# A decode layer on one core: key transposes on 4-byte pairs, flat weight loads, and the gate weights on eight DMA engines

## The chip, the cores and the metric

The kernel runs on one core of one Trainium2 chip. The metric is the device time of one execution in microseconds (us). Each kernel is timed beside the kernel before, in the same rounds on the same chip. Kernels of different rounds are compared by their ratios to it, and the text says so.

## The reference

One token of 448 numbers is normalised, attends with 16 query heads to a cache of 8 heads with 65,536 positions of width 256, and goes in parallel through a gated feed-forward block of width 1,792. Everything is bf16.

```python
x  = A_x                                    # 1 x 1 x 448
xn = layernorm(x)
# attention: q = xn @ wq (448 x 4096); each kv head serves two query heads
scores = einsum("bhqd,bhkd->bhqk", q, k) * 256 ** -0.5      # k, v: 8 x 65536 x 256 each
attn   = einsum("bhqk,bhkd->bhqd", softmax(scores), v) @ wo  # wo: 4096 x 448
# feed-forward on the same token
y = (silu(xn @ w_gate) * (xn @ w_up)) @ w_down               # gate, up: 448 x 1792
return x + attn + (xn + y * sigmoid(xn @ w_r))
```

K and V together are 2 x 8 x 65,536 x 256 x 2 bytes = 536.9 MB, out of 549.0 MB read. Every byte is used once, so this is a kernel that reads.

## The kernel before

One queue, issued by SyncE, brings everything into a ring of 172 KB per partition, in the order of a list of items: `wq`, then K and V pieces of 4 MB (64 positions per partition) alternating one head apart, with gate, up, down and `wo` put in between. An item is loaded as soon as the ring space that it overwrites is free. Each 4 MB transfer is cut into 128 packets of 32,768 bytes, one for each partition, and sixteen DMA engines carry eight packets each. The semaphore of an item receives one increment from each engine that carried part of it; the trace keeps the time of each, so every transfer has a vector of sixteen *landings*. An engine's *lag* is its landing less the first one of the same transfer; the *spread* is the largest lag.

```python
def rows_dmas(src, n, off):                 # wq, gate, up: 448 rows = 3 x 128 + 64
    d = []
    if nfull:                               # 384 rows, three to a partition
        d.append((lambda a, s=src: (a[:, off:off + nfull * n].rearrange("p (k n) -> p k n", k=nfull),
                                    s[0:nfull * P, :].rearrange("(k p) n -> p k n", p=P))))
    if rem:                                 # 64 rows on partitions 0-63 only
        d.append((lambda a, s=src: (a[0:rem, off + nfull * n:off + (nfull + 1) * n], s[nfull * P:D, :])))
    return d
# [...]
def v_next():                               # order of the stream
    v = vs.pop(0)
    if v[3] + v[4] == NPP and v[2] < Hkv - 1 or v[2] == Hkv - 1 and v[3] == sum(V_LAST[:WO_LAST]):
        wo_item(v[2])                       # wo rows of a head, ahead of its last V piece
    kv_item(*v)
    if v[2] == 0 and v[3] == 2 * V_CHUNKS[0]:
        item("ffn1", 2 * DK * F, rows_dmas(B_w_gate, F, 0) + rows_dmas(B_w_up, F, DK * F))
# [...]
def pe_T(n, s, m, j):                       # 16 positions x 128 partitions of keys are one set;
    # [...]                                 # a set takes four of these calls
    kv = ap_of(n).rearrange("p (j d) -> p j d", d=Dh)
    for hf in range(NH):                    # NH = 2 halves of the head width
        for jj in range(GN):                # GN = 4
            blk = hf * GN + jj
            ins = nc.tensor.matmul(ps_t[g % NTB][:, blk * P:(blk + 1) * P],
                                   lhsT=kv[:, j + GN * m + jj, hf * P:(hf + 1) * P],
                                   rhs=ident_bf[:, :], is_transpose=True, start=True, stop=True)
# [...]
def pe_QK(s):                               # scores of the set, from the transposed keys
    # [...]
    ins = nc.tensor.matmul(ps_q[32 * m:32 * m + rep, 0:512],
                           lhsT=qT_sb[:, hf, h * rep:(h + 1) * rep],
                           rhs=kt[:, hf * 512:(hf + 1) * 512],
                           start=(hf == 0), stop=(hf == NH - 1), tile_position=(0, 32 * m))
```

TensorE (PE) first transposes the keys (an identity matmul for each 128 x 128 block), VectorE (DVE) and ScalarE (ACT) copy the result out of PSUM, and PE multiplies it with the queries. V needs no transpose.

## Time and profile before

| | before |
|---|---|
| time, median of 3 runs | 1310.78 us (1310.16 to 1310.97) |
| PE, DVE, ACT busy | 70%, 41%, 33% of the span |
| DMA busy | 9 tenths or more in 39 of 40 slices |
| read rate, slices without weights | about 430 GB/s |
| PE instruction fetches | 107 packets of 16 KB |

The page of the profile of before follows, cut. The rows under the busy shares cut the span into 40 equal slices: the digit is the busy tenths, the GB/s what the DMA engines moved. The two queue lines give packets, megabytes and share of the sixteen engines' time. After them comes the chain of waits that ended last, then the costliest group of PE (count, then busy us, mean ns of one, and idle time ahead).

```profile
span 1309.1 us, 29128 instructions
PE 921.8 (70%) x13690; PEld 701.4 (54%) x13690; DVE 537.7 (41%) x885; ACT 426.6 (33%) x555; POOL 4.5 (0%) x34
...
DMA  9999999999999999999999999999999999999995
GB/s 383 426 427 429 415 382 432 430 430 431 431 430 425 432 428 430 431 428 431 430 430 427 429 429 430 430 430 430 428 428 429 428 426 433 429 429 416 434 426 213
...
q8 instruction: 107, 1.75, 0.5%
...
DMA 75%; PE 25%; SPq 0%; issue 0%; DVE 0%
...
L370 PE MATMUL ps_t<-ident_bf,ring 128*128 128x128 bf16 x8192 | 598.1, 241 | 309.8 <-DMA ring<-in_A_k_cache_dram 308.0
```

The DMA row says what bounds the kernel: the engines of the stream never rest, and the chain is DMA for three quarters. PE, at 70%, spends 309.8 us idle ahead of transposes, waiting for keys. So only what the stream itself loses can be won: slices 5 and 6 (gate, up and down, 415 and 382 GB/s), the first slice (`wq`, 383), and the last (213).

The last slice is the largest. The landings explain it. These are the landings of the sixteen engines for the last transfer of the stream (sorted, in us after the first engine):

```
before, last V piece   0.0 0.02 0.12 0.16 0.19 0.22 0.33 2.44 | 15.76 15.79 16.01 16.05 16.31 17.3 17.43 18.07
```

For the first pieces of the stream all sixteen lie within 0.4 us. By the end, eight engines lag 16 to 18 us behind the first. The slow eight are those that also carry PE's instruction fetches: the queue line has 107 packets of 16 KB, and each adds about 1.55 us to the lag of one engine. It can be seen piece by piece: in those that end at 218.1, 227.8, 237.5 and 247.2 us, with one fetch between each and the next, the lags sum to 28.2, 29.6, 31.2 and 32.9 us, and each time one engine of the slow eight has moved. PE's stream has about 27,390 instructions, which is 107 x 256. The Trainium skill ("Runtime: NRT & Kernel Launch", Instruction fetch mechanics) says that instructions are refilled in 16 KiB blocks of 256 instructions; the trace agrees with the size. The page adds that the cost of a block is "mostly hidden". No wait of PE on the page is put down to it ("issue" is 0% of the chain), but the stream, which ends with its slowest engine, does pay.

How PE does one set of transposes, and the end of the chain, in the profile of before (start us, duration us, what, and the number of instructions):

```profile
61.73 0.60 PE L398 MATMUL ps_q<-kt_buf,qT_sb 128*2 128x512 bf16 x8
62.27 1.96 PE L370 MATMUL ps_t<-ident_bf,ring 128*128 128x128 bf16 x32
```

```profile
1258.10 45.19 DMA ring<-in_A_v_cache_dram
1303.33 0.63 PE ps_o L658 x4
1303.98 0.70 DVE ob_sb L511
1305.24 1.66 PE ps_m L557 x4
1306.93 0.61 DVE res_bf L543
```

A set is 32 transposes in 1.96 us. After the last V piece come four matmuls, a cast, and four matmuls with `wo` (L557, 1.66 us).

### The profile page before, as it was taken

The numbers are of one execution on the slowest core, as the hardware profiler recorded it, in microseconds if no ns is written. First come the engines' busy times: TensorE is split into PE (matmuls) and PEld (weight loads), VectorE is DVE, ScalarE is ACT, GpSimd is POOL, SyncE is SP. The second block draws the span as 40 slices with busy tenths as digits, with TensorE's granted clock in tenths as the row PEclk, the third lists the DMA queues.
The fourth block names the chain that finished last, engine by engine and source line by source line (L and its number), as shares of the span: only waits on it lengthen the run. The fifth ranks groups of instructions, "written<-read, shape, count | busy, mean of one in ns | idle before, by whom it ended". The sixth has DMA issues, their size and how long they took to land.

```text
span 1309.1 us, 29128 instructions
## 1 busy us (share of the span) xinstructions
PE 921.8 (70%) x13690; PEld 701.4 (54%) x13690; DVE 537.7 (41%) x885; ACT 426.6 (33%) x555; POOL 4.5 (0%) x34
## 2 busy tenths in 40 slices
PE   5998765867866767667767668667677577676444
PEld 5886654645645645555556556456456455555210
DVE  3776432434524534335334344345344353353100
ACT  2666322333323423324233233233233242333100
POOL 1000000000000000000000000000000000000000
PEclk9999878878879888788788788788788887888666
DMA  9999999999999999999999999999999999999995
GB/s 383 426 427 429 415 382 432 430 430 431 431 430 425 432 428 430 431 428 431 430 430 427 429 429 430 430 430 430 428 428 429 428 426 433 429 429 416 434 426 213
DMA packets 24701, 550.89 MB, mean 421 GB/s; under 512 B 2371, under 2 KB 6214, under 8 KB 7366
## 3 DMA queue, kind: packets, MB, share of 16 engines
q1 hardware_dynamic: 24578, 549.04, 98.4%
q8 instruction: 107, 1.75, 0.5%
q14 instruction: 12, 0.10, 0.0%
q10 hardware_dynamic: 4, 0.00, 0.0%
HBM read 549.03 MB, written 0.00 MB: 419 GB/s over the span
## 4 chain that ended last, share of the span: by engine, by line
DMA 75%; PE 25%; SPq 0%; issue 0%; DVE 0%
DMA ring<-in_A_k_cache_dram 68%; PE ps_t L370 17%; DMA ring<-in_A_v_cache_dram 7%; PE ps_q L398 4%; PE ps_o L658 2%; PE ps_s L431 1%; PE ps_m L557 0%; SPq L298 0%; PE ps_m L608 0%; PE ps_m L531 0%; DVE ob_sb L511 0%; DVE res_bf L543 0%; PE ps_m L502 0%; DVE oT_sb L518 0%
## 5 line engine op out<-in xcount | busy, mean ns | idle before, releaser
L370 PE MATMUL ps_t<-ident_bf,ring 128*128 128x128 bf16 x8192 | 598.1, 241 | 309.8 <-DMA ring<-in_A_k_cache_dram 308.0
L370 PEld LDWEIGHTS ps_t<-ident_bf,ring 128*128 128x128 bf16 x8192 | 552.0, 110 | 423.8 <-DMA ring<-in_A_k_cache_dram 336.1
L352 DVE COPY kt_buf<-ps_t 128x1024 bf16<-128x1024 bf16 x768 | 493.2, 686 | 636.9 <-PE ps_t L370 636.2
L354 ACT ACTIVATE kt_buf<-ps_t 128x1024 bf16<-128x1024 bf16 x256 | 262.1, 1024 | 431.0 <-PE ps_t L370 430.1
L383 ACT ACTIVATE s<-ps_q 98x512 bf16<-98x512 f32 x256 | 152.9, 597 | 335.5 <-PE ps_q L398 335.5
L658 PE MATMUL ps_o<-ring,S_sb 128*4 128x512 bf16 x2048 | 136.6, 412 | 48.1 <-DMA ring<-in_A_v_cache_dram 46.1
L398 PE MATMUL ps_q<-kt_buf,qT_sb 128*2 128x512 bf16 x2048 | 167.9, 407 | 0.0
L658 PEld LDWEIGHTS ps_o<-ring,S_sb 128*4 128x4 bf16 x2048 | 49.3, 89 | 122.1 <-DMA ring<-in_A_v_cache_dram 54.3
L431 PE MATMUL ps_s<-sel_bf,s 128*128 128x8 bf16 x1024 | 64.9, 169 | 0.7 <-ACT s L383 0.7
L431 PEld LDWEIGHTS ps_s<-sel_bf,s 128*128 128x128 bf16 x1024 | 57.2, 102 | 2.4 <-ACT s L383 1.6
L511 DVE CAST ob_sb<-ps_o 100x512 bf16<-100x512 f32 x8 | 5.5, 692 | 83.7 <-PE ps_o L658 83.7
L398 PEld LDWEIGHTS ps_q<-kt_buf,qT_sb 128*2 128x2 bf16 x2048 | 26.2, 79 | 5.5
L477 ACT ACTIVATE S_sb<-S_sb,negmax 128x512 bf16<-128x512 bf16 x16 | 13.4, 861 | 7.3 <-DVE negmax L470 7.2
L585 PE MATMUL ps_m<-xnT_sb,ring 128*128 128x1 bf16 x112 | 8.1, 175 | 8.8 <-DMA ring<-in_B_w_up_dram 8.8
L585 PEld LDWEIGHTS ps_m<-xnT_sb,ring 128*128 128x128 bf16 x112 | 7.2, 106 | 10.1 <-DMA ring<-in_B_w_up_dram 9.3
L689 PE MATMUL ps_m<-xnT_sb,ring 128*128 128x1 bf16 (+1 forms) x128 | 9.2, 174 | 4.3 <-DMA ring<-in_A_wq_dram 4.3
L411 DVE CAST S_sb<-ps_s 128x512 bf16<-128x512 f32 x16 | 10.9, 682 | 1.3 <-PE ps_s L431 1.3
L413 DVE TENSOR_REDUCE m1p<-S_sb 128x2 f32<-128x512 bf16 x16 | 11.0, 686 | 0.6
L689 PEld LDWEIGHTS ps_m<-xnT_sb,ring 128*128 128x128 bf16 (+1 forms) x128 | 8.3, 106 | 5.3 <-issue 4.4
L557 PE MATMUL ps_m<-ring,oT_sb 128*1 128x448 bf16 x32 | 8.4, 390 | 1.9 <-DVE oT_sb L518 1.9
L502 PEld LDWEIGHTS ps_m<-rowsum,ones_f 128*128 128x128 f32 x32 | 5.8, 256 | 5.1 <-issue 5.1
L570 DVE TENSOR_TENSOR gs_sb<-ps_m,sg_sb 128x14 f32<-128x14 f32 x1 | 0.2, 173 | 18.5 <-ACT sg_sb L565 18.5
(63 smaller groups left out, 62.3 us busy)
## 6 DMA issues: line engine op xcount, KB each, us to landing
ring<-in_A_k_cache_dram SPq DMA_DIRECT2D x63, 4096.0 KB, 44.3
ring<-in_A_v_cache_dram SPq DMA_DIRECT2D x63, 4096.0 KB, 37.9
ring<-in_A_wo_dram SPq DMA_DIRECT2D x8, 448.0 KB, 30.3
ring<-in_A_wq_dram SPq DMA_DIRECT2D x1, 3072.0 KB, 10.4
ring<-in_A_k_cache_dram SPq DMA_DIRECT2D x2, 1024.0 KB, 15.1
ring<-in_A_k_cache_dram SPq DMA_DIRECT2D x1, 2048.0 KB, 21.8
ring<-in_A_v_cache_dram SPq DMA_DIRECT2D x1, 2048.0 KB, 41.6
ring<-in_B_w_down_dram SPq DMA_DIRECT2D x1, 1568.0 KB, 34.4
```

The lines of the kernel that those rows point to most:

```text
L352: op(e, ("EV", g), lambda x: x.tensor_copy(out=kt[:, :], in_=tb[:, :]))
L354: op(e, ("EV", g), lambda x: x.activation(out=kt[:, :], in_=tb[:, :], func=ACTF.Copy))
L370: ins = nc.tensor.matmul(ps_t[g % NTB][:, blk * P:(blk + 1) * P], lhsT=kv[:, j + GN * m + jj, hf * P:(hf + 1) * P], rhs=ident_bf[:, :], is ...
L383: op("act", ("EVQ", s), lambda e: e.activation(out=s2[s % 2][0:QROWS, :], in_=ps_q[0:QROWS, :], func=ACTF.Copy))
L398: ins = nc.tensor.matmul(ps_q[32 * m:32 * m + rep, 0:512], lhsT=qT_sb[:, hf, h * rep:(h + 1) * rep], rhs=kt[:, hf * 512:(hf + 1) * 512], s ...
L411: op("dve", ("SCOPY", b), lambda e: e.tensor_copy(out=S[:, k * SBN:(k + 1) * SBN, :], in_=ps_s[:, :, :]))
L413: op("dve", ("SMAX", b), lambda e: e.tensor_reduce(out=m1p[:, h % 2, :, k], in_=S[:, k * SBN:(k + 1) * SBN, :].rearrange("p n i -> p i n") ...
L431: ins = nc.tensor.matmul(o, lhsT=s2[s % 2][:, jj * P:(jj + 1) * P], rhs=sel_bf[:, :, :], start=True, stop=True)
L477: op("act", ("EXPI", h, i), lambda e, i=i: e.activation(out=S[:, :, i], in_=S[:, :, i], func=ACTF.Exp, bias=negmax[:, h, i:i + 1], scale=1 ...
L585: ins = nc.tensor.matmul(ps_m[0:P, base + f:base + f + 1], lhsT=w[0:r, t, kc, f * P:(f + 1) * P], rhs=xnT_sb[0:r, kc:kc + 1], start=(kc == ...
L658: ins = nc.tensor.matmul(ps_o[32 * g:32 * g + 2 * rep, :], lhsT=S[:, k:k + 2, :].rearrange("p n i -> p (n i)"), rhs=kv[:, j:j + 2, :], sta ...
L689: ins = nc.tensor.matmul(ps_m[0:P, c:c + 1], lhsT=w[0:r, kc, q * Dh + hf * P:q * Dh + (hf + 1) * P], rhs=xnT_sb[0:r, kc:kc + 1], start=(kc ...
```

## The change

The intent is to take work from the DMA stream, and from its slow engines above all. There are four parts.

1. **Transposes on 4-byte pairs** (`t4`). Two neighbouring bf16 keys are treated as one fp32, so one transpose moves a 128 x 256 block instead of two that move 128 x 128 each: 4,096 instead of 8,192. The two halves of the head width become even and odd elements, and the scores matmul reads every second column.
2. **Flat weights** (`flat`). `wq`, gate and up are loaded as one contiguous run for each of 128 partitions (3.5 of the 448 rows each), and `w_down` in runs of two rows. No remainder on half the partitions, and longer packets. PE then multiplies with permuted columns of x, prepared by ten small DVE operations.
3. **Gate on eight engines** (`SPREAD`). The gate's source is written with an outer dimension of 8, so that eight engines carry it. The intent is to give these bytes to the eight engines that are ahead.
4. **Last two `wo` items at the end of the stream** (`WO_END`), behind the last V piece.

The ring also shrinks, from 172 to 169 KB per partition.

```diff
+SPREAD = True
+WO_END = 2
@@ loads
+    def flat_dma(src, n, off, spread):
+        def d(a):
+            dst = a[:, off:off + RP * n // 2]
+            v = src.rearrange("a b -> (a b)")
+            if spread:
+                return dst, v.rearrange("(u a n) -> a u n", a=8, u=P // 8)
+            return dst, v.rearrange("(p n) -> p n", p=P)
         return d
-    item("wq", DK * HqDh, rows_dmas(A_wq, HqDh, 0))
+    item("wq", RP * HqDh // 2, [flat_dma(A_wq, HqDh, 0, False)])
-            item("ffn1", 2 * DK * F, rows_dmas(B_w_gate, F, 0) + rows_dmas(B_w_up, F, DK * F))
+            item("ffn1", RP * F, [flat_dma(B_w_gate, F, 0, SPREAD), flat_dma(B_w_up, F, RP * F // 2, False)])
@@ order of the stream
-        if v[3] + v[4] == NPP and v[2] < Hkv - 1 or v[2] == Hkv - 1 and v[3] == sum(V_LAST[:WO_LAST]):
+        if v[3] + v[4] == NPP and v[2] < Hkv - WO_END:
             wo_item(v[2])
+    for h in range(Hkv - WO_END, Hkv):
+        wo_item(h)
@@ transposes and scores
-        kv = ap_of(n).rearrange("p (j d) -> p j d", d=Dh)
-        for hf in range(NH):
-            for jj in range(GN):
-                blk = hf * GN + jj
-                    ins = nc.tensor.matmul(ps_t[g % NTB][:, blk * P:(blk + 1) * P],
-                                           lhsT=kv[:, j + GN * m + jj, hf * P:(hf + 1) * P],
-                                           rhs=ident_bf[:, :], is_transpose=True, start=True, stop=True)
+        kv = ap_of(n).bitcast(FP32).rearrange("p (j d) -> p j d", d=P)
+        for jj in range(GN):
+                ins = nc.tensor.matmul(ps_tf[g % NTB][:, jj * P:(jj + 1) * P], lhsT=kv[:, j + GN * m + jj, :],
+                                       rhs=ident_f[:, :], is_transpose=True, start=True, stop=True)
-                                           rhs=kt[:, hf * 512:(hf + 1) * 512],
+                                           rhs=kt[:, :].rearrange("p (k f) -> p f k", f=NH)[:, hf, :],
@@ [cut: flat_mm, which multiplies with the flat weights; pe_attn_end, the eight last wo matmuls;
@@  the permuted columns of x on DVE and ACT; w_down's layout, two rows of 448 a run instead of one]
```

## The prediction

> **What bounds it now.** The DMA stream. The 40-slice view shows DMA at 9 tenths in all slices but the last, at about 430 GB/s; PE is busy 70%, DVE 41%, ACT 33%. In the chain of waits 75% is DMA. All 549 MB must still be read, so only what the stream loses can be won: the last slice (213 GB/s, about 16 us lost), the weight slices (415, 382), the first (383).
>
> The trace's landing records (one per DMA engine and transfer) show why: eight engines run away from the other eight. Between first and last engine of one 4 MB transfer lie 0.4 us at the start and 18.1 us at the end. The slow eight also fetch instructions: the queue table has 107 "instruction" packets (16 KB, 1.07 us each), each adding about 1.55 us to one engine's lag. 107 x 256 is PE's instruction count. So the slowest engine carries 13 to 14 fetches, about 20 us.
>
> **What the change does to the slow engines.**
> - Transposes 8192 -> 4096 (each a weight load and a matmul): PE's stream falls from about 27,390 to 19,160 instructions, 107 -> 75 fetches, 4 fewer per slow engine: -6 us.
> - wq flat: its 64-row remainder fills half the partitions, where packets take 616 ns instead of 309: -1.5 us. Gate and up likewise, and their 3584 B rows take 151 ns (23.7 GB/s against 27.0 for 32 KB): -3.3 us. w_down (896 B, 41 ns): -0.6 us.
> - Gate on 8 engines: the Trainium skill ("DMA: Bandwidth & Descriptors", Why a DMA increments its semaphore by 16) says the lowest-numbered 8 are used, and a 128-partition transfer gives engines 0-7 partitions 0-63 (The descriptor swizzle). The trace agrees that the fast ones are 0-7: 32 KB packets of the engines ahead take 1.9 us, not 1.215, while laggards still write the remainder to partitions 0-63. So the gate falls on the right half. That takes 100 KB, 3.7 us, off each slow engine; but half its rows still enter by their partitions, and the doubled packets say a port passes no more than one engine's rate. I count 0 for the slow eight, and 4 to 11 us of delay for the fast eight, which have it to spare.
> - Two wo items last: V lands 2.4 us earlier and its chain (cast, transposes, 1.9 us) runs under them, but eight matmuls follow instead of four: -1 us.
> - Ten small DVE operations before the first transpose: about 2 us, hidden behind wq.
>
> Sum: about -12.5 us, all at the stream's end, on the critical path.
>
> **PE.** The existing 4-byte transposes of the maxima are single-pass (one record each, 270 ns against 219). 4-byte 128x128 weight loads follow each other at 110 ns. So 16 transposes per set take 1.8 us if load and matmul overlap, against 1.96 us for 32; 3.5 us if not. A K and a V transfer last 19.4 us together; PE needs 13.5, so the second case would be PE-bound near 1400 us. Strided keys may double the 0.6 us of the scores matmuls; that fits.
>
> **Prediction: 1298 us, 1291 to 1304.** Faster by over 2%: 2%; within: 91%; slower: 7%.
>
> **Signs.** About 75 instruction packets; spread at the end 8 us or less; last slice above 213 GB/s; no dip at the weights; transposes x4096 near 110 ns apart; last V landing near 1289 us.
>
> **Wrong if** 4-byte loads do not hide (PE above 90%), the gate's engines are the slow half (+4 to 10 us), or ports pass more than I think (-3 us).

## More of the kernel before

The stretch of the gate load in before, with busy time and instructions of each engine, the granted PE clock, the DMA share and the rate:

```profile
core 0: us, PE busy (x) PEld busy (x) DVE busy (x) ACT busy (x) POOL busy (x), PEclk, DMA share, GB/s
160.00:180.00 20.00, 11.19 (x185) 8.80 (x183) 4.00 (x7) 4.87 (x6) 0.00 (x0) 0.77 1.03 359
```

## The result

| | before | after |
|---|---|---|
| median | 1310.88 us (4 runs, 1310.16 to 1311.03) | 1312.38 us (4 runs, 1309.84 to 1312.70) |
| ratio | | 1.0008 (95%: 0.9991 to 1.0026) |

No change, against a predicted gain of 12.5 us: the time is outside the predicted range of 1291 to 1304. A ratio in this document is the mean time of one kernel's runs over that of the other's of the same rounds, so it is not quite the ratio of the medians quoted beside it. A ratio turned into microseconds is taken of 1310 us.

The page of the profile of after, the same lines:

```profile
span 1310.5 us, 20912 instructions
PE 922.5 (70%) x9576; PEld 694.6 (53%) x9576; DVE 539.0 (41%) x895; ACT 432.4 (33%) x559; POOL 4.5 (0%) x34
...
DMA  9999999999999999999999999999999999999994
GB/s 400 430 430 430 384 335 433 431 427 432 431 430 429 429 430 429 431 429 431 431 431 431 428 430 430 431 430 429 428 430 429 431 423 430 430 430 431 431 430 205
...
q8 instruction: 75, 1.23, 0.4%
...
DMA 73%; PE 26%; another core or an unknown queue 1%; SPq 0%; issue 0%; DVE 0%
...
L374 PE MATMUL ps_t<-ident_f,ring 128*128 128x128 f32 x4096 | 602.3, 310 | 302.1 <-DMA ring<-in_A_k_cache_dram 300.3
```

Much came as predicted: 75 fetches instead of 107, the first slice at 400 GB/s instead of 383, and PE busy for the same 922 us with half the transposes. But slices 5 and 6, where the weights are, fell from 415 and 382 to 384 and 335, and the last slice is no better (205). A set and its scores on PE, and the end of the chain, in the profile of after:

```profile
62.41 0.63 PE L401 MATMUL ps_q<-kt_buf,qT_sb 128*2 128x512 bf16 x8
62.97 1.97 PE L374 MATMUL ps_t<-ident_f,ring 128*128 128x128 f32 x16
```

```profile
1258.66 44.79 DMA ring<-in_A_v_cache_dram
1303.50 0.63 PE ps_o L694 x4
1304.15 0.70 DVE ob_sb L514
1305.17 3.09 PE ps_s L562 x8
1308.28 0.61 DVE res_bf L547
```

Sixteen 4-byte transposes take 1.97 us, what 32 of the others took. The strided scores matmuls take 0.63 us instead of 0.60. Neither is a new limit. The last V piece still lands at 1303.5 us, where it landed before (1303.3).

The stretch of the gate, in the profile of after (columns as for before):

```profile
160.00:180.00 20.00, 5.88 (x80) 3.60 (x78) 3.75 (x6) 4.04 (x5) 0.00 (x0) 0.76 1.01 241
```

This is the line to look at twice. The DMA share is 1.01: the engines are busy all the time. But they move 241 GB/s instead of 359. A busy engine is not a working one. The durations of the packets in the records of the DMA engines between 150 and 182 us show why (ns, at 10%, 50% and 90% of the packets; those of 12,544 bytes are both gate and up):

```
            packet     count   10%    50%    90%
before       3584 B     896    140    151    266     gate and up, rows of 1792
            32768 B     274   1213   1218   1509     keys and values
after       12544 B     256    732    928    976     gate and up, flat
            32768 B     180   1213   1221   2408     keys and values
e1          12544 B     256    469    473    479     gate on 16 engines
            32768 B     319   1213   1218   1221
```

The same 12,544-byte packet takes about 0.93 us in after and 0.47 us where the gate goes over sixteen engines (experiment e1, below), and the 32 KB packets beside it take up to 2.4 us instead of 1.2. The landings of the last transfer are these:

```
after, last wo item    0.0 0.43 | 3.66 4.03 4.04 4.24 6.83 9.65 9.68 9.83 9.86 10.51 10.61 11.38 | 19.17 19.52
```

Two engines end 7.8 us behind the other fourteen. Over the gate the spread grew from 3.6 to 11.0 us, where the prediction expected it to shrink.

### The profile page after: what moved, and what is told of

Same layout as the page of the kernel before. It is cut to its first block, busy times and chain, and to the rows that moved or that the text cites. A ratio compares the mean times of both kernels' runs of the same rounds, so it can differ in the third digit from the quotient of the medians.

```text
span 1310.5 us, 20912 instructions
## 1 busy us (share of the span) xinstructions
PE 922.5 (70%) x9576; PEld 694.6 (53%) x9576; DVE 539.0 (41%) x895; ACT 432.4 (33%) x559; POOL 4.5 (0%) x34
## 4 chain that ended last, share of the span: by engine, by line
DMA 73%; PE 26%; another core or an unknown queue 1%; SPq 0%; issue 0%; DVE 0%
DMA ring<-in_A_k_cache_dram 66%; PE ps_t L374 18%; DMA ring<-in_A_v_cache_dram 6%; PE ps_q L401 4%; PE ps_o L694 2%; PE ps_s L434 1%; PE ps_m L579 0%; SPq L304 0%; PE ps_m L644 0%; PE ps_s L562 0%; PE ps_m L534 0%; PE ps_m L505 0%; DVE ob_sb L514 0%; DVE res_bf L547 0%
## 5 line engine op out<-in xcount | busy, mean ns | idle before, releaser
L374 PE MATMUL ps_t<-ident_f,ring 128*128 128x128 f32 x4096 | 602.3, 310 | 302.1 <-DMA ring<-in_A_k_cache_dram 300.3
L374 PEld LDWEIGHTS ps_t<-ident_f,ring 128*128 128x128 f32 x4096 | 536.2, 161 | 419.1 <-DMA ring<-in_A_k_cache_dram 328.6
L401 PE MATMUL ps_q<-kt_buf,qT_sb 128*2 128x512 bf16 x2048 | 173.5, 417 | 0.0
L434 PEld LDWEIGHTS ps_s<-sel_bf,s 128*128 128x128 bf16 x1024 | 67.8, 102 | 7.6 <-ACT s L386 1.6
L607 PE MATMUL ps_m<-xnT_sb,ring 128*128 128x2 bf16 x210 | 8.5, 179 | 18.0 <-DMA ring<-in_B_w_up_dram 16.4
L480 ACT ACTIVATE S_sb<-S_sb,negmax 128x512 bf16<-128x512 bf16 x16 | 13.4, 863 | 5.3 <-DVE negmax L473 5.3
## 6 DMA issues: line engine op xcount, KB each, us to landing
ring<-in_A_k_cache_dram SPq DMA_DIRECT2D x2, 1024.0 KB, 13.4
```

Of the source, the lines that this page charges most:

```text
L374: ins = nc.tensor.matmul(ps_tf[g % NTB][:, jj * P:(jj + 1) * P], lhsT=kv[:, j + GN * m + jj, :], rhs=ident_f[:, :], is_transpose=True, sta ...
L401: ins = nc.tensor.matmul(ps_q[32 * m:32 * m + rep, 0:512], lhsT=qT_sb[:, hf, h * rep:(h + 1) * rep], rhs=kt[:, :].rearrange("p (k f) -> p ...
L434: ins = nc.tensor.matmul(o, lhsT=s2[s % 2][:, jj * P:(jj + 1) * P], rhs=sel_bf[:, :, :], start=True, stop=True)
L480: op("act", ("EXPI", h, i), lambda e, i=i: e.activation(out=S[:, :, i], in_=S[:, :, i], func=ACTF.Exp, bias=negmax[:, h, i:i + 1], scale=1 ...
L607: ins = nc.tensor.matmul(o, lhsT=cols(a, rr * width, c), rhs=X[:, x0:x0 + 2], start=(b == 0), stop=(b == RP * half - 1), skip_group_check= ...
```

## The experiments

Twelve experiments ran (e1_again repeats the kernel of e1). All gave correct results. In the expectations the theories have letters: A, that the gate's eight-engine load is to blame, in two forms: the eight meet each other at the ports into the memory of the core (A1), or they meet the traffic of the other eight, or a load on eight engines costs this anyhow (A2); and as rival (B), that another part of the change costs what the rest wins (the flat loads, the 4-byte transposes).

### e1_no_spread: the change without part 3

```diff
-SPREAD = True
+SPREAD = False
```

> The changed kernel with the gate weights on all 16 DMA engines, all else kept. Theory A (the gate load on 8 engines throws away bandwidth, because the eight write to partitions whose ports are in use): the 384 and 335 GB/s of the slices at the weights go back to 420 or more, 32 KB packets there stay near 1.22 us, the spread of the engines at the end is 12 to 14 us, and the time is 1296 to 1301 us. Rival B (the flat loads or the 4-byte transposes lose it): the slices stay low or the time stays at 1308 us or more.

Measured: 1298.00 us (1297.10 to 1298.48) against 1309.96; ratio 0.9906 (0.9893 to 0.9920). As expected, and also the very number that was predicted for the whole change. The profile of e1, its rates, its fetches and the stretch of the gate:

```profile
GB/s 404 429 430 429 426 433 429 428 432 430 432 425 433 428 430 433 426 430 428 431 430 431 430 429 429 432 429 429 432 428 433 426 433 428 429 434 428 429 433 257
...
q8 instruction: 75, 1.23, 0.4%
```

```profile
160.00:180.00 20.00, 12.05 (x173) 10.34 (x170) 3.04 (x7) 4.68 (x6) 0.00 (x0) 0.70 1.03 438
```

The dip at the weights is gone (426 and 433 in slices 5 and 6), and the stretch moves 438 GB/s instead of 241 at the same DMA share. So the eight-engine gate costs 1.0008 - 0.9906 (different rounds), about 13.4 us, and the three other parts do together what they should. One number missed: the spread at the end is 15.7 us, not 12 to 14.

### e2_t4_only: before with the 4-byte transposes alone

```diff
-        kv = ap_of(n).rearrange("p (j d) -> p j d", d=Dh)
+        kv = ap_of(n).bitcast(FP32).rearrange("p (j d) -> p j d", d=P)
+        [one transpose of fp32 for each two of bf16; scores and wq columns strided, as in the change]
```

> The kernel before with only the 4-byte transposes (16 per set for 32). If instruction fetches on eight engines are what makes them late: 75 or 76 packets for 107, spread at the end 12 to 14 us for 18, time 1304 to 1306.5 us. If the fetches are innocent, or the PE does not keep up: 1310 us or more.

Measured: 1305.63 us (1304.51 to 1306.52) against 1309.96; ratio 0.9965 (0.9952 to 0.9977), so -4.6 us. It has 75 fetches, and its spread at the end is 15.9 us (18.1 before), not the expected 12 to 14. The rival theory, that these transposes cost what the rest wins, falls: they win.

### e4_gate_4x32 and e5_gate64: two builds that did not do what they should

Both should load the gate with eight engines in such a way that the engines don't meet: e4 in four transfers of 32 partitions, e5 on partitions 0 to 63 only.

```diff
# e4
+            v = B_w_gate.rearrange("a b -> (a b)").rearrange("(p n) -> p n", p=P)
+            return a[32 * b:32 * b + 32, 0:RP * F // 2], v[32 * b:32 * b + 32, :].rearrange("(e w) n -> e w n", e=8)
# e5
+                v = src.rearrange("(p r) n -> p (r n)", p=HP)[32 * b:32 * b + 32, :]        # HP = 64
+                return a[32 * b:32 * b + 32, off:off + RP * n], v.rearrange("(e w) n -> e w n", e=8)
```

> The gate on 8 engines as in the change, the same bytes to the same 128 partitions, but as four loads of 32 partitions, so that each of the eight engines writes 4 neighbouring partitions per load[...]. Theory A1 (the eight collide among themselves): half of the gate packets take about 0.47 us, the other half, in partitions 64 to 127, up to twice that against the other engines' stream; time 1298 to 1304 us. Theory A2 (only the collision with the other eight engines counts, or eight engines for one load cost this anyhow): 1309 us or more, like the changed kernel.

> The gate on 8 engines, but laid into partitions 0 to 63 only (two loads of 32 partitions, twice the bytes per partition, seven whole rows in each). If it is the port that counts, the eight write to their own ports and the other eight go on undisturbed: no 32 KB packet over 1.8 us at the weights beyond those beside a fetch, each gate packet of 25 KB near 0.94 us, spread at the end 5 to 9 us, time 1291 to 1297 us. If limiting a load to 8 engines is what costs: 1300 us or more.

Measured: e4 1304.18 us (1303.81 to 1306.00), ratio 0.9959 (0.9946 to 0.9971); e5 1306.15 us (1305.25 to 1306.74), ratio 0.9968 (0.9955 to 0.9982); both against 1309.96. They miss their expectations, but they don't test the theory: the trace has sixteen landings for each of these loads, so sixteen engines carried it. The gate load of after has nine: eight, and one for the rest of the count. The Trainium skill ("DMA: Bandwidth & Descriptors", Why a DMA increments its semaphore by 16 and not by 1) says that the number of engines is the largest k up to 16 that divides the slowest dimension of both sides, and that the remaining increments come at once. That agrees with the nine landings of after. In e4 and e5 the source, 8 blocks of 4 rows that follow each other without a gap, may count as one dimension of 32 rows, of which sixteen is a divisor; that reading is argued from the sixteen landings, from the next two kernels, and from the records of the load instructions, which have the destination of e4 and e5 as [32,1], one dimension, and that of e4b and e5b as [1,32]. So they show something else: sixteen engines pushing into 32 partitions. In e4 the 12,544-byte packets took 0.92 us at the median and 1.34 us at the 90% mark, against 0.47.

### e4b_gate_4x32 and e5b_gate64: the same, with eight engines

Interleaving the rows ("u e" instead of "e w") leaves a stride that cannot be merged. Each engine then takes rows that are eight apart, and the columns of x are permuted to match. Both have eight engines in the trace.

```diff
# e4b: four transfers, partitions 0-31, 32-63, 64-95, 96-127
+            return a[32 * b:32 * b + 32, 0:RP * F // 2], v[32 * b:32 * b + 32, :].rearrange("(u e) n -> e u n", e=8)
# e5b: two transfers, partitions 0-31 and 32-63; runs of seven rows, 25088 B
+                return a[32 * b:32 * b + 32, off:off + RP * n], v.rearrange("(u e) n -> e u n", e=8)
```

> The first try of this (e4) ran on 16 engines: each load had 16 landings, as neighbouring rows were merged. Here the rows are interleaved, so each of the four loads should have 8 landings. Same bytes and the same 128 partitions as the changed kernel, 8 engines, but engine a writes only partitions 4a to 4a+3 of each 32. Theory A1 (the eight hinder each other, two at one port, in the changed kernel): the gate packets for partitions 0 to 63 take about 0.47 us, those for 64 to 127 about 0.94, and the time is 1296 to 1301 us. Theory A2 (it is the other eight engines' traffic that they meet): nearly all gate packets still take 0.9 us and the time is 1306 us or more.

> As e5, now really on 8 engines and into partitions 0 to 63 only. Port theory: 16 gate packets of 25 KB per engine pair, each near 0.94 us, 32 KB packets at the weights stay near 1.22 us, the spread of the engines falls after the gate instead of growing, end spread 8 to 10 us, time 1293 to 1296 us, under e1 by 3 to 4. If the eight engines that get it are the slow ones: above e1, 1301 us or more. If limiting a load to 8 engines costs in itself: 1298 us or more.

Measured: e4b 1306.04 us (1305.93 to 1309.33), ratio 0.9976 (0.9964 to 0.9989); e5b 1300.34 us (1300.24 to 1301.68), ratio 0.9927 (0.9914 to 0.9939); both against 1310.47.

Packets are told apart here by their order in time. In e4b those of the first two transfers, to partitions 0 to 63, take 0.47 us (up to 160.2 us of the span), and those of the last two, to partitions 64 to 127, 0.95 us, with 32 KB packets beside them at up to 2.5 us. In e5b every packet is clean: 25,088 bytes in 0.93 us, twice the size in twice the time, and 32 KB in 1.22 us at the 90% mark. In packets e4b did what A1 said, in time what A2 said: by their partitions no two of the eight meet any more, yet it wins back only a third of what e1 does (0.9976 and 0.9906, against 1.0008 for after). Half of its gate still meets the other eight. The stretch of the gate in e5b moves nearly what e1 moves:

```profile
160.00:180.00 20.00, 12.53 (x211) 10.85 (x207) 2.48 (x4) 3.65 (x5) 0.00 (x0) 0.71 1.01 431
```

This settles the first cause: engines that meet at the same partitions make each other's packets take twice as long. The Trainium skill ("DMA: Bandwidth & Descriptors", The descriptor swizzle) gives engines 0 to 7 the partitions 0 to 63 of a 128-partition transfer and engines 8 to 15 the others; "SBUF — State Buffer" (Door 1: The DMA port swizzle) says that each port serves eight partitions. The trace agrees as far as it can show it: 0.47 us for 12,544 bytes and 0.93 us for 25,088 where, by these pages, each engine stays on its own partitions (the first half of e4b, and e5b), and twice that in the half of e4b that goes to partitions of the other eight.

But e5b is still about 2.7 us slower than e1 (ratios of 0.9927 and 0.9906, from different rounds; the intervals overlap slightly). In its own rounds it is slower than e7 (below, e1 without the move of `wo`), and no run of the one overlaps the other. It should have been faster, for it was meant to take bytes from eight engines and give them to the engines that are ahead. Its spread *grew* over the gate, from 3.2 to 11.0 us. These are the landings of the 4 MB piece before the gate, of the one after it, and of the last transfer, which has the shape of after's:

```
e5b, piece before      0.0 0.09 0.2 0.26 0.37 0.51 0.92 1.13 | 1.62 1.68 1.79 1.86 2.28 3.17 3.23 3.24
e5b, piece after       0.0 0.25 | 1.43 1.51 1.6 2.91 2.96 2.98 | 7.19 7.26 7.37 7.55 8.12 8.33 | 10.37 11.0
e5b, last wo item      0.0 0.07 | 2.5 3.0 3.0 3.42 6.18 8.97 9.15 9.22 9.36 10.63 10.69 10.73 | 16.35 17.15
```

Before the gate there are eight engines ahead and eight behind. In the piece after it, the two at the left are engines that are ahead and did not get the gate; then come six that are behind and did not get it, and six that were ahead and did. The two at the right are engines that were behind and did get it. If the gate's eight had been the eight that are ahead, there would be no such corners. So the eight engines of the gate are six of the fast ones and two of the slow ones. That is the second cause, and a step of the prediction that was wrong. By the time alone, the last branch of the expectation, that a load on eight engines costs in itself, would fit as well; the table of mean landings below speaks against it, for e5b loses no engine time against e1.

### e6b_gateup64: gate and up on eight engines

```diff
-UP64 = False
+UP64 = True        # on top of e5b: up as well, on partitions 0-63 by the same eight engines
```

> Gate and up both on 8 engines into partitions 0 to 63, which shifts twice as much. Port theory: another 3 to 4 us off e5b, 1289 to 1293 us, end spread 4 us or so by pairs of engines. If the stream is then bound by something common to all engines: no better than e5b.

Measured: 1305.36 us (1304.04 to 1305.46) against 1310.47; ratio 0.9959 (0.9946 to 0.9973). It misses the 1289 to 1293 that it was hoped to reach, and confirms the misaiming by doubling it: the two engines at the right now end 8.6 us behind the other fourteen (in the last transfer 18.4 and 19.1 us after the first, the rest at 9.8 or less).

### e7_wo_back: e1 with `wo` where it was

```diff
-SPREAD = True
-WO_END = 2
+SPREAD = False
+WO_LAST = 7
+        [order of wo, its matmuls and the last addition as in before]
```

> e1 with the last two wo items put back where they were. If moving them is worth what I reckoned: 1 us more than e1, 1298.5 to 1300 us, and the time from the last V landing to the end shrinks to 5.7 us from e1's, while the last landing comes 2.4 us later. If it is worth nothing: equal to e1 within 0.5 us.

Measured: 1298.94 us (1298.75 to 1299.39) against 1310.47; ratio 0.9913 (0.9900 to 0.9927). e1's ratio of 0.9906 is 0.9 us less, so the move of `wo` wins about 1 us, as predicted (the intervals overlap; the two kernels were not in the same rounds). The chain of e7 and that of e1 end like this:

```profile
1247.27 43.89 DMA ring<-in_A_v_cache_dram
1291.20 0.63 PE ps_o L673 x4
1291.85 0.70 DVE ob_sb L512
1293.12 1.67 PE ps_m L558 x4
1294.81 0.61 DVE res_bf L544
```

```profile
1289.52 0.70 DVE ob_sb L514
1290.52 2.60 PE ps_s L562 x8
1293.14 0.61 DVE res_bf L547
```

The cast (ob_sb) starts 2.3 us earlier in e1, since two loads no longer stand ahead of the last V piece, and eight matmuls in 2.60 us replace four in 1.67 us.

### e3_flat_only: before with the flat weights alone

```diff
-SPREAD = True
-WO_END = 2
+SPREAD = False
+WO_LAST = 7
+        [transposes, scores and wo as in before]
```

> The kernel before with only the flat loads of wq, gate, up (16 engines) and the longer rows of w_down; 2-byte transposes, wo as before. By my sum -5.4 us: 1304 to 1306 us, 107 packets, spread at the end as before (18 us). By the difference of the runs so far (e7 less e2) -6.7 us: 1303 to 1304.5 us. If the two parts are not independent: 1307 us or more.

Measured: 1305.49 us (1304.75 to 1305.76) against 1310.28; ratio 0.9962 (0.9949 to 0.9976), so -5.0 us, where -5.4 was predicted. The fetches are 107 as before, and its slices 5 and 6 are at 424 and 432 GB/s. Flat loads win by themselves.

The three parts alone sum to -4.6 - 5.0 - 0.9 = -10.5 us, and together (e1) they give -12.3. The 1.8 us more than the sum are left open.

### e8_gate_k4: the gate on the four lowest engines

If two of the engines 0 to 7 are slow, a smaller k may hold only fast ones. The gate goes over four engines, on partitions 0 to 15 and 32 to 47, which by the descriptor swizzle cited above are those of engines 0 to 3 in a 128-partition transfer.

```diff
+                v = src.rearrange("(p r) n -> p (r n)", r=RG)[16 * b:16 * b + 16, :]      # RG = 14
+                return a[32 * b:32 * b + 16, off:off + RG * n], v.rearrange("(u e) n -> e u n", e=4)
```

> The gate on 4 engines (0 to 3, landings 4 per load) in partitions 0 to 15 and 32 to 47[...]; about 1.2 packets of instructions more than e1. e5b showed two late engines among the eight that got the gate. If both are among engines 4 to 7: the four that get it were early, all late ones are relieved by 3.7 us, time 1293 to 1296 us, under e1. If one or both are among 0 to 3: they get 11 us more, end last, time 1303 to 1310 us. Clean ports in both cases: packets of 50 KB near 1.87 us.

Measured: 1300.05 us (1299.80 to 1300.23) against 1310.28; ratio 0.9922 (0.9910 to 0.9935). It misses 1293 to 1296. The packets are clean (50,176 bytes in 1.855 us), and the landings of the 4 MB pieces before and after the gate are these (in us after the first):

```
e8, piece before       0.0 0.11 0.17 0.19 0.21 0.34 0.75 1.17 | 1.47 1.48 1.5 1.9 2.41 3.04 3.11 3.19
e8, piece after        0.0 0.07 0.09 0.22 | 1.36 1.38 1.79 2.28 2.9 2.93 2.98 3.07 | 14.72 14.91 15.46 15.89
```

Four early, eight late as before, four gated: all eight slow engines are among those without the gate. So the gated four are all of the fast kind, and if they are engines 0 to 3 and the gate's eight were 0 to 7, as "DMA: Bandwidth & Descriptors" of the Trainium skill has it in the section cited at e4 (on the SyncE queue the lowest-numbered k are taken; the trace shows only how many), the two slow ones are among 4 to 7. And the spread at the end, 13.3 us, is smaller than in any run before it. Yet it isn't the fastest. The profile of e8 suggests the reason, in PE's timeline (in brackets the idle time ahead and what ended it; the item of the gate and up ends with up; the first line is cut by the end of its window), in SyncE's longest wait for it (total us, times, longest us) and in the stretch after the gate:

```profile
177.04 3.14 PE L627 MATMUL ps_m<-xnT_sb,ring 48*128 48x1 bf16 x56 [12.16 <-DMA ring<-in_B_w_up_dram]
187.58 2.77 PE L618 MATMUL ps_m<-xnT_sb,ring 128*128 128x2 bf16 x49
```

```profile
SPq L315 <- PE ps_m L618: 25.1, 1, 25.1
```

```profile
180.00:200.00 20.00, 20.00 (x284) 18.55 (x283) 7.00 (x13) 5.05 (x8) 0.00 (x0) 0.67 0.79 327
```

Four engines need so long for the gate that it lands late. PE meets it in its program order and waits 12.16 us. Then it needs 10.6 us for the gate alone, since this layout takes 196 matmuls of one column for it (e1 does gate and up with 98 in 5.4 us), and 2.8 us for up (L618). Only then does it free ring space: SyncE waits 25.1 us for it, the other twelve engines run out of work, and the DMA share falls to 0.79. So about half of the stall lies in the wait for the late landing and half in the matmuls that follow; no run here separates the two.

### e9_gate_k4_late: e8 with the gate's matmuls four steps later

```diff
-                pe_ffn1(n)
+                defer(4, lambda n=n: pe_ffn1(n))
```

> e8 aimed well (its four engines, late by 15 us after the gate, ended before the late eight), yet took 1300 us: in its slice at the weights the engines were busy 79% only, as PE waits for the late gate, frees nothing, and the engines that are ahead run out of work. Here PE first works through the next key item (about 10 us) and then takes the gate. If that wait is what e8 lost: the DMA share at 180 to 200 us rises towards 1, time 1294 to 1298 us. If the ring, a third of which the gate holds, is the limit anyhow: 1299 us or more.

Measured: 1321.67 us (1321.01 to 1322.37) against 1310.05; ratio 1.0086 (1.0072 to 1.0099). A miss, the slowest of all: the DMA share at 180 to 200 us falls to 0.43 instead of rising. In the trace of e9, PE waits 22.63 us for keys, and SyncE issues nothing for 48 us. The fences show PE's and SyncE's timelines and SyncE's longest wait (total us, times, longest us):

```profile
187.65 3.67 PE L385 MATMUL ps_t<-ident_f,ring 128*128 128x128 f32 x16 [22.63 <-DMA ring<-in_A_k_cache_dram]
```

```profile
165.06 0.39 SPq L315 DMA_DIRECT2D ring<-in_B_w_down_dram  x1
213.65 0.33 SPq L315 DMA_DIRECT2D ring<-in_A_k_cache_dram  x1
```

```profile
SPq L315 <- PE ps_m L618: 48.2, 1, 48.2
```

Putting off the gate's matmuls (196 here too) doesn't help, since the next key piece lies behind the gate in the queues of the same four engines, and a piece is complete only when all sixteen have landed. And L618 is the matmuls of up, the last of the feed-forward item: its ring space is freed only after them, four steps later, and until then the issue of new loads stands still. A load that only few engines carry delays everything behind it in the same queue.

### e1_again

The kernel of e1, unchanged, beside e9.

> The version with the gate on all 16 engines once more, on the same chip as e9, to compare the two: 1297 to 1299 us.

Measured: 1297.91 us (1297.62 to 1298.22) against 1310.05; ratio 0.9905 (0.9892 to 0.9919). The best version is thus the change with `SPREAD = False`, 0.95% under before, repeated on a second chip.

## Why the prediction was wrong

The total, 1298 us, was missed by 14 us, and one term of its sum is the cause: the gate, booked at 0. The mean over the sixteen landings of the last transfer says how much engine time the stream took; the distance from that mean to the last landing says how unevenly it was spread. Both are worked out from the landings of one profiled run of each kernel (us from the start of the span):

```
           mean landing    last - mean    last landing
before       1293.73           9.56         1303.29
after        1294.52          11.18         1305.70
e1           1283.70           7.60         1291.30
e4b          1289.43           9.94         1299.37
e5b          1284.14           9.63         1293.77
e6b          1285.04          13.80         1298.84
e8           1288.39           4.84         1293.23
```

From e1 to after the last landing moves by 14.4 us: 10.8 in the mean, 3.6 in the unevenness. e5b, without collisions, keeps e1's mean within 0.4 us and has 2.0 of the unevenness. e4b, in which half of the gate's packets collide, has 5.7 in the mean, about half of the 10.8. So most of the loss is engine time wasted in collisions; of the 3.6 us of unevenness, the two misaimed engines account for some 2.0 (e5b), and the rest is left open. e6b and e8 test the misaiming from both sides: with twice the bytes on the two slow engines the unevenness grows to 13.8 us, and with the gate on fast engines alone it falls to 4.8 us, while the mean of e8 holds its idle time. e5b also differs from after in the layout of the gate in memory and in the number of its matmuls, but PE is not the limit there.

**Steps that were wrong:**

- *"I count 0 for the slow eight, and 4 to 11 us of delay for the fast eight, which have it to spare."* This is the term that was mis-sized. The prediction had the mechanism (two engines at one port share its rate), and had seen it in the trace (32 KB packets at 1.9 us). But it booked the collision to the engine that comes from outside alone. A collision doubles the packets of both parties: the 32 KB packets beside the gate took up to 2.4 us for about 20 us. In the first 4 MB piece after the gate, the six slow engines without the gate land at 182.5 to 184.1 us in after, and the slow eight at 175.9 to 177.7 us in e1: 6 to 7 us later, where 0 was counted; without collisions (e5b) they land at 172.3 to 173.8 us. Measured, the gate on eight engines costs 13.4 us (after against e1) where the prediction counted 0; 10.8 us of the 14.4 us in the profiles are in the mean, as the table shows.
- *"So the gate falls on the right half."* Six of the eight engines were fast, two slow (e5b, e6b, e8). The evidence, doubled 32 KB packets, only showed that *some* of the engines that are ahead use partitions 0 to 63. It was read as if all did. The cost, 2.7 us between the ratios of e1 and e5b, is smaller than the 4 to 10 us named for the case that all eight were slow.
- *"spread at the end 8 us or less"* was 19.5 us in after, and 15.7 us even in e1. Without the gate change, fewer fetches take two microseconds off the spread, not ten. This sign was to come mostly from the gate.

**Steps that held:**

- The DMA stream bounds the kernel, and what the stream saves arrives at the end: e1, e2 and e3 all show it.
- 107 to 75 fetches. The win was sized at 6 us and measured at 4.6 us (e2).
- Flat weights: sized at 5.4 us, measured at 5.0 us (e3); the dip at the weights goes (e1).
- The moved `wo`: sized at 1 us, measured at 0.9 us.
- The 4-byte transposes hide their weight loads: a set was sized at 1.8 us and took 1.97 us, against 1.96 us before. PE stayed at 70%; the strided keys cost 0.03 us a set.
- The DVE operations ahead of the first transpose make the q projection start later (15.09 instead of 13.93 us), and it still ends sooner: its 112 matmuls take 3.15 us, the 128 of before took 9.22 us. Why they follow each other so much faster I did not pursue; the time isn't on the stream's path.
- The gate was booked at 0, so the predicted sum of about 12.5 us is that of the other terms, and it met e1's 1298.0 us exactly. That is partly chance: the transposes won 1.4 us less than they were sized at, and the parts won 1.8 us more together than alone.

## What to carry to other kernels

A DMA engine that is 100% busy may be colliding: look at the time of equal packets and at the rate of a stretch, not at the busy share, and when you take a load from some engines, make sure that the others write only to partitions that are theirs, for a collision slows both parties. In a stream that ends with its slowest engine, read the sixteen landings of a late transfer first: fewer instructions on the busiest engine's program shorten the stream even where that engine is not the limit. And before you steer bytes to the engines that are ahead, identify each of them by a test, not by half.

## What the Trainium skill lacked or had wrong

- "Runtime: NRT & Kernel Launch" (Instruction fetch mechanics) says that the cost of a 16 KiB block is "mostly hidden". For PE the profile shows no wait for it. For a DMA-bound stream it isn't: each block delays one data engine by about 1.55 us, and 32 fewer blocks made this kernel 4.6 us faster (e2).
- No page says which of the data engines carry PE's instruction fetches. Here eight of sixteen do, and they end 16 to 18 us after the first engine (before); by the page's numbering of a small k, none of engines 0 to 3 is among them, two of 4 to 7 are (e5b, e8), and so six of 8 to 15.
- "DMA: Bandwidth & Descriptors" (Why a DMA increments its semaphore by 16 and not by 1) gives the rule for the number of engines but not that rows which follow each other without a gap may count as one dimension: an outer dimension of 8 over contiguous rows still ran on sixteen engines (e4, e5: 16 landings), and an interleaved one on eight (e4b, e5b).
- The same page gives no price for a transfer on fewer than sixteen engines that writes to partitions of all ports: 12,544-byte packets went from 0.47 to 0.93 us, 32 KB packets beside them from 1.2 to 2.4 us, and the rate of the stretch from 438 to 241 GB/s (e1 and after).
- "TensorE: Matmul & The Clock Gate" (Part 4: PE-mode transpose) gives durations for 128 x 128 bf16 alone, none for 4-byte elements. Here sixteen fp32 transposes of 128 x 128 with their weight loads took 1.97 us, 32 bf16 ones 1.96 us.
